# All scores of the next attention pair in one TensorE visit, over six PSUM banks, and four more weight conversions in the first batch

## The chip, the cores and the metric

The kernel runs on one core of one Trainium2 chip. The metric is the device time of one execution in microseconds (us). The engines are TensorE (PE, with its weight loads listed apart as PEld), VectorE (DVE), ScalarE (ACT), GpSimd (POOL) and SyncE (SP, which issues the DMAs).

## The reference

Four batches of eight heads, 576 tokens, head size 64, all float32. The result of the attention, as a matrix of 2304 tokens by 512, goes through a gated feed-forward block:

```python
scores = scale * np.matmul(q, k.transpose(0, 1, 3, 2))        # causal mask, minus row maximum
a = np.exp(scores); a /= a.sum(-1, keepdims=True) + 1e-09
local = np.matmul(a, v)
q_p = phi(q)                                                  # phi(x) = max(x, 0) + exp(min(x, 0))
mem_out = einsum(q_p, M_prev) / (einsum(q_p, z_prev) + 1e-6)
attn = g * mem_out + (1 - g) * local                          # g = sigmoid(beta), one per head
x = attn.transpose(0, 2, 1, 3).reshape(2304, 512)
out = ((x @ w1) * (x @ w2)) @ w3 @ w_out                      # w1, w2: 512x1024, w3: 1024x1024, w_out: 1024x512
```

The weights come to the chip as float64 numbers, seen as pairs of 32-bit words, and are converted to float32 there.

## The kernel before

**Pairs.** Two heads form a pair; there are 16 pairs, four to a batch. The q and k of a pair lie on the 128 partitions as two halves of 64 (`a` = 0 and 1), so a score matmul uses half of the array's rows, one head each. The 576 query tokens are cut into c = 0 (64 rows, both heads together, `s_mm0`) and c = 1 to 4 (128 rows each, for both heads), whose causal rows are 64, 192, 320, 448 and 576 keys long. For each c the scores go to PSUM, are read by DVE (`s_red`, L179: mask added, negative maximum taken, result to the SBUF tile `sm`), go through the exponential on ACT (`s_exp`, L217, which also sums), and are scaled by DVE (`s_norm`, L221 to L226). PE then transposes `sm` (`t_mm`, L236, L257), ACT copies the transposes to `pt` (L267), and PE forms the product with v (`pv_mm`, L283) in the PSUM tile `x`, to which `mem_mm` (L273, L274) has already written the memory part. `fin` (L293 on ACT, L294 on DVE) splits `x` into a high and a low part in `xs`. The memory part needs `mem_a`, `mem_b`, `mem_c` on ACT, DVE and POOL and five transposes on PE (`mem_t`, L162).

**PSUM.** `ps_t` has four banks, used in turn for scores and transposes. `ps_x` is one tile of two banks, which serves the transposes of `mem_t` and the output `x` of a pair. `ps_m` has two banks for the fill described next.

**Fill.** Attention alone leaves PE free for much of the time. So other matmuls are woven in: the string `ORDER` gives the steps of a pair (transposes, product and end of pair p, scores and softmax of pair p + 1), and each `F` in it is a slot in which a generator puts in its share of matmuls. In the first batch the generator is `w_gen` (L413: w3 times w_out). In batches 2 to 4 it is `moe_gen` of the batch before: `gemm1` (L447, twelve matmuls of 288 columns to a PSUM bank, evicted by ACT at L453 and multiplied in by DVE at L456, after which ACT and POOL split the product at L458 and L459) and `gemm2` (L467, 24 matmuls of 512 columns to a bank). The last batch's feed-forward runs alone at the end.

**Conversion.** Forty jobs convert the weights, each by ACT (L315), DVE (L319, L320) and, for w1 and w2, ACT and POOL again (L327, L328). `conv_tick` moves all jobs on by a stage; a slot calls it when `tick_ok` allows. In the first batch it allows jobs up to `limit`; after it, all.

A scheduler orders the instructions of each engine from this program order and priorities; each engine then works through its own list in order and waits on semaphores.

Of the kernel before, what the change touches and what calls it, by code (L numbers as in the profile page):

```python
# [21 lines left out]
    "lqn t2 F "  # L22
    "t3a F "
    "th t3b F "
    "s321 ma F "
    "e3 mb F "
    "n3 t4a F "
    "e2 e1 t4b t5 F "
    "n2 s4 mc F "
    "e4 F "  # L30
    "mm s0 e0 n4 F "
    "pv lq F "
    "fin F "
).split()
# [7 lines left out]
def attention_moe_kernel(  # L42
# [13 lines left out]
    nc = tc.nc  # L56
# [129 lines left out]
    def s_group(p, jobs):  # L186
        t = raw_t[p]
        red = []
        for group in jobs:
            xs = [bank(), bank()]  # L190
            o = 0
            for c, lo, hi in group:
                for a, x in enumerate(xs):
                    r = slice(64 * a, 64 * a + 64)
                    nc.tensor.matmul(x[:, o:o + hi - lo], lhsT=t[r, 0, 128 * c - 64:128 * c + 64], rhs=t[r, 1, lo:hi], start=True, stop=True)  # L195
                    red.append((c, a, x[:, o:o + hi - lo], lo, hi))
                o += hi - lo
        for c, a, x, lo, hi in red:
            s_red(p, c, a, x, lo, hi, lo == 0)

    def s_mm4(p):
        s_group(p, [[(4, 0, 288)], [(4, 288, 576)]])

    def s_mm321(p):
        s_group(p, [[(3, 0, 448)], [(2, 0, 320), (1, 0, 192)]])

    def s_mm0(p):
        x = bank()
        nc.tensor.matmul(x[:, 0:64], lhsT=qd, rhs=raw_t[p][:, 1, 0:64], start=True, stop=True)
        s_red(p, 0, 0, x[:, 0:64], 0, 64)  # L210

# [85 lines left out]
    def conv_stages(k, src, dh, dl):  # L297
# [15 lines left out]
        def scale():  # L313
            box["p"] = dh() if k < 24 else o_p.tile([128, n], F32, tag="o", name="wp")
            nc.scalar.activation(out=box["p"], in_=f32(box["raw"][:, :, 1]), func=ACTF.Prelu, scale=2.0 ** -111, alpha=-(2.0 ** 32))  # L315
# [50 lines left out]
    limit = [28]  # L366
# [149 lines left out]
    def pair_step(p, F):  # L516
# [13 lines left out]
            s4=(nx, lambda: s_mm4(p + 1)),  # L530
            s321=(nx, lambda: s_mm321(p + 1)),
            s0=(nx, lambda: s_mm0(p + 1)),
# [6 lines left out]
            n2=(nx, lambda: s_norm(p + 1, 4, 8)),  # L539
            n4=(nx, lambda: (s_norm(p + 1, 0, 2), s_norm(p + 1, 8, 9))),  # L540
# [45 lines left out]
    s_mm321(0)  # L586
# [3 lines left out]
    s_norm(0, 2, 8)  # L590
    conv_tick()
    s_mm4(0)
    s_mm0(0)
    s_exp(0, 4)
    s_exp(0, 0)
    s_norm(0, 0, 2)
    s_norm(0, 8, 9)
# [49 lines left out]
```

## Time and profile before

| what | value |
|---|---|
| median of 3 runs | 594.22 us (592.11, 594.22, 594.63) |
| the profiled execution | 592.49 us, span 590.7 us from the first to the last instruction |
| mean granted TensorE clock | 0.974 of full speed |
| busy | PE 557.9 us, PEld 441.2, DVE 288.5, ACT 279.7, POOL 125.5 |

The profile shows one execution, the 592.49 us one; its span leaves out about 1.8 us before the first and behind the last instruction. A PE line in the timeline joins neighbouring matmuls of one line; "x12" counts records, and a float32 score matmul leaves two records (two passes). Record ends are modelled, so the distance from start to start tells more than a length.

### The profile page before, as it was taken

The page shows a single profiled execution, that of the slowest core. Times are in us where ns is not written, and L with a number is a line of the kernel's source. Part 1 is how long each engine was busy: PE and PEld are TensorE (multiplying, and loading weights), DVE is VectorE, ACT ScalarE, POOL GpSimd, SP SyncE. Part 2 cuts the span into 40 slices and gives each one's busy share as a digit, 9 for nine tenths or more (in the row PEclk, how much of TensorE's full clock was granted, in tenths as well). Part 3 has the DMA queues.
Part 4 walks back from the last instruction along what each step waited for, and adds up shares of the span by engine and source line. Part 5 has one row for each costly group of instructions (what it writes and reads, how often), then busy time and mean ns, then how long its engine had stood idle before and what let it go on. Part 6 is the DMA issues. An engine that isn't in the chain of part 4 may idle for free.

```text
span 590.7 us, 9323 instructions
## 1 busy us (share of the span) xinstructions
PE 557.9 (94%) x3440; PEld 441.2 (75%) x3440; DVE 288.5 (49%) x910; ACT 279.7 (47%) x723; POOL 125.5 (21%) x153
## 2 busy tenths in 40 slices
PE   4499979999699999999999999999999999999997
PEld 2344445456589798878897888788887988898995
DVE  5967978765844536263636262626363531111111
ACT  4745857456735355544544464425452743121220
POOL 1201232114612022211330122103120311121220
PEclk8689999999899999999999999999999999999999
DMA  7983453506111121113111203040303000000001
GB/s 272 403 346 94 148 182 125 177 20 173 36 43 50 62 68 32 59 29 110 41 54 34 91 4 89 22 132 6 88 6 122 2 23 19 18 2 19 19 1 53
DMA packets 23070, 48.31 MB, mean 82 GB/s; under 512 B 6897, under 2 KB 13041, under 8 KB 21489
## 3 DMA queue, kind: packets, MB, share of 16 engines
q1 hardware_dynamic: 23024, 47.72, 24.3%
q8 instruction: 27, 0.44, 0.3%
q14 instruction: 19, 0.15, 0.1%
HBM read 43.00 MB, written 4.72 MB: 81 GB/s over the span
## 4 chain that ended last, share of the span: by engine, by line
PE 77%; DVE 11%; ACT 6%; POOL 2%; DMA 2%; issue 2%; SPq 0%; DVEq 0%; ACTq 0%
PE m L447 31%; PE m L467 17%; PE x L283 7%; PE s L236 7%; PE m L413 6%; PE s L195 6%; PE x L274 2%; ACT sm L217 2%; DVE sm L179 2%; DVE sm L226 2%; PE x L162 1%; POOL e L143 1%; DVE qn L141 1%; DMA wst<-w_out 1%; DVE wp L320 1%
## 5 line engine op out<-in xcount | busy, mean ns | idle before, releaser
L447 PE MATMUL m<-xs,wsp 128*128 128x288 f32 x1536 | 230.1, 302 | 5.2 <-DVE a L456 5.0
L447 PEld LDWEIGHTS m<-xs,wsp 128*128 128x128 f32 x1536 | 209.4, 190 | 11.5 <-DVE a L456 5.5
L217 ACT ACTIVATE sm<-sm,mx 128x448 f32<-128x448 f32 (+2 forms) x144 | 82.8, 576 | 80.5 <-DVE mx L179 80.4
L459 POOL TENSOR_TENSOR ht<-a,ht 128x288 fp32r<-128x288 f32 (+2 forms) x96 | 57.2, 607 | 273.0 <-ACT ht L458 272.9
L467 PE MATMUL m<-wH,ht 128*128 128x512 f32 x288 | 98.5, 402 | 0.0
L267 ACT ACTIVATE pt<-s 128x512 f32<-128x512 f32 (+1 forms) x144 | 65.9, 487 | 32.3 <-PE s L236 26.2
L456 DVE SCALAR_TENSOR_TENSOR a<-m,a 128x288 f32<-128x288 f32 x64 | 29.1, 455 | 97.3 <-PE m L447 97.2
L236 PE MATMUL s<-ident,sm 128*128 128x128 f32 x448 | 68.9, 282 | 4.8 <-DVE sm L226 4.8
L179 DVE CUSTOM_DVE_ANT_0 sm<-s,mask 128x448 f32<-128x448 f32 (+2 forms) x144 | 58.4, 448 | 22.1 <-PE s L195 20.5
L236 PEld LDWEIGHTS s<-ident,sm 128*128 128x128 f32 x448 | 56.8, 146 | 16.0 <-issue 12.5
L413 PE MATMUL m<-wo,w3s 128*128 128x512 f32 x128 | 66.0, 635 | 1.7 <-DVE w3s L320 1.7
L467 PEld LDWEIGHTS m<-wH,ht 128*128 128x128 f32 x288 | 54.1, 188 | 13.4 <-issue 2.6
L195 PE MATMUL s<-raw 64*128 64x288 f32 (+3 forms) x320 | 56.2, 455 | 8.0 <-DMA raw<-qkt 4.4
L226 DVE TENSOR_SCALAR sm<-sm,sums 128x448 f32<-128x448 f32 (+2 forms) x144 | 62.4, 476 | 1.8
L458 ACT ACTIVATE ht<-a 128x288 fp32r<-128x288 f32 (+2 forms) x96 | 31.2, 356 | 56.8 <-DVE a L456 56.8
L467 PE MATMUL m<-wL,ht 128*128 128x512 f32 x144 | 56.4, 392 | 0.0
L195 PEld LDWEIGHTS s<-raw 64*128 64x128 f32 x320 | 30.6, 191 | 32.3 <-issue 11.7
L143 POOL TENSOR_TENSOR e<-qn,z 128x640 f32<-128x640 f32 x16 | 25.2, 1572 | 120.1 <-DVE qn L141 120.1
L283 PE MATMUL x<-pt,v 128*64 128x448 f32 (+4 forms) x384 | 46.7, 392 | 0.0
L283 PEld LDWEIGHTS x<-pt,v 128*64 128x64 f32 x384 | 25.1, 137 | 25.7 <-issue 21.1
L453 ACT ACTIVATE a<-m 128x288 f32<-128x288 f32 x64 | 25.8, 404 | 37.9 <-PE m L447 32.2
L413 PEld LDWEIGHTS m<-wo,w3s 128*128 128x128 f32 x128 | 22.7, 200 | 20.0 <-issue 17.6
(62 smaller groups left out, 427.5 us busy)
## 6 DMA issues: line engine op xcount, KB each, us to landing
raw<-qkt SPq DMA_DIRECT2D x16, 576.0 KB, 3.8
wst<-w3t SPq DMA_DIRECT2D x8, 1024.0 KB, 12.2
wst<-w SPq DMA_DIRECT2D x16, 512.0 KB, 4.4
qn<-qn SPq DMA_DIRECT2D x16, 320.0 KB, 3.0
v<-v SPq DMA_DIRECT2D x32, 160.0 KB, 2.3
out<-o SPq DMA_DIRECT2D x18, 256.0 KB, 2.0
wst<-w_out SPq DMA_DIRECT2D x4, 1024.0 KB, 9.4
z<-z_prev SPq DMA_DIRECT2D x16, 64.0 KB, 2.8
```

Of the source, the lines that this page charges most:

```text
L179: nc.vector.tensor_tensor_reduce(out=sm[a][c][:, lo:hi] if c else sm0[:, 0:64], in0=x, in1=mask[:, S - KE[c] + lo:S - KE[c] + hi] if c els ...
L195: nc.tensor.matmul(x[:, o:o + hi - lo], lhsT=t[r, 0, 128 * c - 64:128 * c + 64], rhs=t[r, 1, lo:hi], start=True, stop=True)
L217: nc.scalar.activation(out=x, in_=x, func=ACTF.Exp, bias=mx, scale=-1.0, accum_out=sums_of(p)[:, k:k + 1])
L226: nc.vector.tensor_scalar(out=x, in0=x, scalar1=sums_of(p)[:, k:k + 1], scalar2=None, op0=ALU.mult)
L236: tr = lambda o, c, a, kc: nc.tensor.transpose(ps[:, o:o + 128], sm[a][c][:, 128 * kc:128 * kc + 128], ident)
L267: nc.scalar.activation(out=d, in_=s, func=ACTF.Copy)
L283: nc.tensor.matmul(x[64 * a:64 * a + 64, 384 + q0:384 + q1], lhsT=vv[:, a, kc], rhs=pt[:, a, o:o + q1 - q0], start=False, stop=(q0 == 0 or ...
L413: nc.tensor.matmul(ps, lhsT=w[:, 128 * kc:128 * kc + 128], rhs=wo[:, 512 * (kc % 2):512 * (kc % 2) + 512], start=(kc == 0), stop=(kc == 7))
L447: nc.tensor.matmul(ps[:, 0:U], lhsT=w[:, i, x, j], rhs=x_t[NC * b + j][:, xx, U * u:U * u + U], start=(k == 0), stop=(k == 11))
L458: nc.scalar.activation(out=hbuf(f, 0)[:, p:p + c], in_=a[:, o:o + c], func=ACTF.Copy)
L459: nc.gpsimd.tensor_tensor(out=hbuf(f, 1)[:, p:p + c], in0=a[:, o:o + c], in1=f32(hbuf(f, 0)[:, p:p + c]), op=ALU.subtract)
L467: nc.tensor.matmul(ps, lhsT=hbuf(f, a)[:, p:p + 128], rhs=b[f], start=(k == 0), stop=(k == 23))
```

## The change

In `ORDER`, the scores of the next pair were computed at three places: `s321` (c = 3, 2, 1 over four banks), `s4` (c = 4 as two times 288 columns over four banks) and `s0`. Now there is one step `ss`, behind `mm`, `pv` and `fin` of the current pair: c = 4 as 512 + 64 columns and c = 3 in the four banks of `ps_t`, and c = 2 and 1 in the two banks of `ps_x` (tile `sx`), which become free when `fin` has read `x`; then `s_mm0`. The exponentials and normalisations of the next pair follow in the six slots from there to the first transposes `t1`, in the order c = 4, 3, 2, 1, 0; the transposes of the current pair are moved together at the front. The prologue for the first pair follows the same order. Apart from this, `limit` goes from 28 to 32, and the jobs k = 26, 27, 30, 31, 34 and 35 take their buffer `wp` from the pool `big` instead of the pool `o`.

```diff
--- before.py
+++ after.py
@@ -19,18 +19,18 @@
 
 ORDER = (
     "lv mt t1 F "
-    "lqn t2 F "
-    "t3a F "
-    "th t3b F "
-    "s321 ma F "
-    "e3 mb F "
-    "n3 t4a F "
-    "e2 e1 t4b t5 F "
-    "n2 s4 mc F "
-    "e4 F "
-    "mm s0 e0 n4 F "
-    "pv lq F "
+    "lqn t2 th F "
+    "t3a t3b F "
+    "t4a F "
+    "t4b t5 F "
+    "mm pv ma F "
     "fin F "
+    "ss lq mb F "
+    "F "
+    "e4 mc F "
+    "n4 e3 F "
+    "n3 F "
+    "e2 e1 e0 n2 F "
 ).split()
 
 
@@ -183,31 +183,27 @@
         )
         stat["mx", p, a, c] = mx
 
-    def s_group(p, jobs):
-        t = raw_t[p]
-        red = []
-        for group in jobs:
-            xs = [bank(), bank()]
-            o = 0
-            for c, lo, hi in group:
-                for a, x in enumerate(xs):
-                    r = slice(64 * a, 64 * a + 64)
-                    nc.tensor.matmul(x[:, o:o + hi - lo], lhsT=t[r, 0, 128 * c - 64:128 * c + 64], rhs=t[r, 1, lo:hi], start=True, stop=True)
-                    red.append((c, a, x[:, o:o + hi - lo], lo, hi))
-                o += hi - lo
-        for c, a, x, lo, hi in red:
-            s_red(p, c, a, x, lo, hi, lo == 0)
-
-    def s_mm4(p):
-        s_group(p, [[(4, 0, 288)], [(4, 288, 576)]])
-
-    def s_mm321(p):
-        s_group(p, [[(3, 0, 448)], [(2, 0, 320), (1, 0, 192)]])
-
     def s_mm0(p):
         x = bank()
         nc.tensor.matmul(x[:, 0:64], lhsT=qd, rhs=raw_t[p][:, 1, 0:64], start=True, stop=True)
         s_red(p, 0, 0, x[:, 0:64], 0, 64)
+
+    def s_all(p):
+        t = raw_t[p]
+        lay = []
+        for a in range(2):
+            lay.append([bank(), bank()])
+        xx = ps_x.tile([128, 1024], F32, tag="x", name="sx")
+        red = []
+        for i, o, c, lo, hi in ((0, 0, 4, 0, 512), (1, 0, 4, 512, 576), (1, 64, 3, 0, 448), (2, 0, 2, 0, 320), (2, 320, 1, 0, 192)):
+            for a in range(2):
+                y = xx[:, 512 * a + o:512 * a + o + hi - lo] if i == 2 else lay[a][i][:, o:o + hi - lo]
+                r = slice(64 * a, 64 * a + 64)
+                nc.tensor.matmul(y, lhsT=t[r, 0, 128 * c - 64:128 * c + 64], rhs=t[r, 1, lo:hi], start=True, stop=True)
+                red.append((c, a, y, lo, hi))
+        for c, a, y, lo, hi in red:
+            s_red(p, c, a, y, lo, hi, lo == 0)
+        s_mm0(p)
 
     def s_exp(p, c):
         for a in range(2 if c else 1):
@@ -311,7 +307,12 @@
             nc.sync.dma_start(out=t[:, 0:2 * n].bitcast(U32), in_=src.bitcast(U32))
 
         def scale():
-            box["p"] = dh() if k < 24 else o_p.tile([128, n], F32, tag="o", name="wp")
+            if k < 24:
+                box["p"] = dh()
+            elif k < 36 and k % 4 > 1:
+                box["p"] = big.tile([128, n], F32, tag=f"r{4 + k % 4}", name="wp")
+            else:
+                box["p"] = o_p.tile([128, n], F32, tag="o", name="wp")
             nc.scalar.activation(out=box["p"], in_=f32(box["raw"][:, :, 1]), func=ACTF.Prelu, scale=2.0 ** -111, alpha=-(2.0 ** 32))
 
         def join():
@@ -363,7 +364,7 @@
     tick = [0]
     nload = [0]
     w_done = [0]
-    limit = [28]
+    limit = [32]
 
     def tick_ok():
         k = tick[0]
@@ -527,17 +528,15 @@
             t1=(1, lambda: t_mm(p, "1")),
             th=(1, lambda: t_mm(p, "h")),
             t5=(1, lambda: t_mm(p, "5")),
-            s4=(nx, lambda: s_mm4(p + 1)),
-            s321=(nx, lambda: s_mm321(p + 1)),
-            s0=(nx, lambda: s_mm0(p + 1)),
+            ss=(nx, lambda: s_all(p + 1)),
             e4=(nx, lambda: s_exp(p + 1, 4)),
             e3=(nx, lambda: s_exp(p + 1, 3)),
             e2=(nx, lambda: s_exp(p + 1, 2)),
             e1=(nx, lambda: s_exp(p + 1, 1)),
             e0=(nx, lambda: s_exp(p + 1, 0)),
             n3=(nx, lambda: s_norm(p + 1, 2, 4)),
-            n2=(nx, lambda: s_norm(p + 1, 4, 8)),
-            n4=(nx, lambda: (s_norm(p + 1, 0, 2), s_norm(p + 1, 8, 9))),
+            n2=(nx, lambda: s_norm(p + 1, 4, 9)),
+            n4=(nx, lambda: s_norm(p + 1, 0, 2)),
             lq=(p + 2 < NP, lambda: load_qk(p + 2)),
             mm=(1, lambda: mem_mm(p)),
             pv=(1, lambda: pv_mm(p)),
@@ -583,18 +582,15 @@
         nc.vector.tensor_copy(out=gis[:, :, 2 * k:2 * k + 2], in_=gp)
     for a in range(2):
         nc.vector.tensor_copy(out=gis[64 * a:64 * a + 64, :, 8], in_=gp[64 * a:64 * a + 64, :, a])
-    s_mm321(0)
+    s_all(0)
+    s_exp(0, 4)
+    conv_tick()
+    s_norm(0, 0, 2)
     for c in (3, 2, 1):
         s_exp(0, c)
         conv_tick()
-    s_norm(0, 2, 8)
-    conv_tick()
-    s_mm4(0)
-    s_mm0(0)
-    s_exp(0, 4)
     s_exp(0, 0)
-    s_norm(0, 0, 2)
-    s_norm(0, 8, 9)
+    s_norm(0, 2, 9)
     load_qk(1)
     mem_a(0)
     mem_b(0)
```

What the scheduler makes of it, on the two engines at which most of the waits of this part are: first PE, from one score visit to the next of a pair beside the feed-forward block (s are the banks of `ps_t`, m those of `ps_m`, numbers in tile names are buffers). Before:

```order
L195 MATMUL s<-raw 128x448 [waits DMAHW4_49,Activation_49]
L195 MATMUL s<-raw 128x448 [waits Activation_49]
L195 MATMUL s<-raw 128x320 [waits PE_49,Activation_49]
L195 MATMUL s<-raw 128x320 [waits Activation_49]
L195 MATMUL s<-raw 128x192 x2
...
L195 MATMUL s<-raw 128x288 [waits DVE_49]
L195 MATMUL s<-raw 128x288 [waits Activation_49] x3
...
L209 MATMUL s<-raw,qd 128x64 [waits DMAHW6_49,DMAHW5_49,DVE_49]
```

Two visits of the row halves, and the 64-column matmul of c = 0 alone, each between fill (the rows left out are L447, L467 and transposes). After, around the visit before pair 9:

```order
L448 MATMUL m<-xs,wsp 128x288 x5
L202 MATMUL s<-raw 128x512 [waits DMAHW6_49,PE_49]
L202 MATMUL s<-raw 128x512 [waits PE_49]
L202 MATMUL s<-raw 128x64 [waits PE_49] x2
L202 MATMUL s<-raw 128x448 x2
L202 MATMUL sx<-raw 128x320 [waits DVE_49]
L202 MATMUL sx<-raw 128x320
L202 MATMUL sx<-raw 128x192 x2
L188 MATMUL s<-raw,qd 128x64 [waits DMAHW7_49,DMAHW0_49,DVE_49]
L448 MATMUL m<-xs,wsp 128x288 x18
L448 MATMUL m<-xs,wsp 128x288 [waits Activation_49]
L448 MATMUL m<-xs,wsp 128x288 x11
```

All ten row-half matmuls and the c = 0 matmul now stand in one place, 21 L448 behind the last product with v (L279); the first one on `sx` waits for DVE, and the fill behind has a wait for ACT after 18 matmuls, at the bank that L454 has to read (L454 is L453 of before, L448 is L447).

Second, ACT in a pair beside the feed-forward block. Before:

```order
L217 ACTIVATE sm_110,sums<-sm_110,mx 128x448 [waits DVE_49]
L217 ACTIVATE sm_114,sums<-sm_114,mx 128x448 [waits DVE_49]
L217 ACTIVATE sm_109,sums<-sm_109,mx 128x320 [waits DVE_49]
L453 ACTIVATE a<-m 128x288 [waits PE_49,Pool_49]
L217 ACTIVATE sm_113,sums<-sm_113,mx 128x320 [waits DVE_49]
L217 ACTIVATE sm_108,sums<-sm_108,mx 128x192 [waits DVE_49]
L217 ACTIVATE sm_112,sums<-sm_112,mx 128x192 [waits DVE_49]
L458 ACTIVATE ht<-a 128x288 [waits DVE_49]
L267 ACTIVATE pt<-s 128x4x128 [waits PE_49]
```

The exponentials of c = 3, 2 and 1 (sm_110, sm_114, sm_109, sm_113, sm_108, sm_112) stood together, with the eviction L453 after three of them; those of c = 4 and 0 came later, behind other evictions and copies. After:

```order
L459 ACTIVATE ht<-a 128x288 [waits DVE_49]
L213 ACTIVATE sm_111,sums<-sm_111,mx 128x576 [waits DVE_49]
L213 ACTIVATE sm_110,sums<-sm_110,mx 128x448 [waits DVE_49]
L213 ACTIVATE sm_115,sums<-sm_115,mx 128x576 [waits DVE_49]
L213 ACTIVATE sm_114,sums<-sm_114,mx 128x448 [waits DVE_49]
L213 ACTIVATE sm_109,sums<-sm_109,mx 128x320 [waits DVE_49]
L454 ACTIVATE a<-m 128x288 [waits PE_49,Pool_49]
L213 ACTIVATE sm_113,sums<-sm_113,mx 128x320 [waits DVE_49]
L213 ACTIVATE sm_108,sums<-sm_108,mx 128x192 [waits DVE_49]
L213 ACTIVATE sm_112,sums<-sm_112,mx 128x192 [waits DVE_49]
L213 ACTIVATE sm_107,sums<-sm_107,mx 128x64 [waits DVE_49]
L459 ACTIVATE ht<-a 128x288 [waits DVE_49]
```

All nine exponentials (L213) now follow each other, c = 4 (sm_111, sm_115) among the first, and one eviction L454 stands among them, behind five.

## Rows read from the trace of the kernel before

**Rows 1.** The page: PE's busy line, and the chain that ended last.

```profile
PE 557.9 (94%) x3440; PEld 441.2 (75%) x3440; DVE 288.5 (49%) x910; ACT 279.7 (47%) x723; POOL 125.5 (21%) x153
...
PE 77%; DVE 11%; ACT 6%; POOL 2%; DMA 2%; issue 2%; SPq 0%; DVEq 0%; ACTq 0%
```

**Rows 2.** Table by windows: start:end, length, busy us of each engine, clock.

```profile
115.79:141.28 25.49, 25.49 (x118) 13.38 (x116) 16.18 (x51) 14.99 (x37) 5.72 (x4) 1.00 0.22 62
141.28:508.60 367.32, 361.93 (x2451) 305.58 (x2450) 170.35 (x565) 179.93 (x482) 81.87 (x100) 0.99 0.18 54
```

**Rows 3.** Waits of PE: us in total, times, longest.

```profile
PE m L447 <- DVE a L456: 5.0, 2, 4.2
```

**Rows 4.** PE timeline, first batch: start us, us, instructions, [idle before].

```profile
29.40 8.06 PE L413 MATMUL m<-wo,w3s 128*128 128x512 f32 x12 [1.70 <-DVE w3s L320]
...
55.16 0.74 PE L162 MATMUL x<-ident,qn 128*128 128x128 f32 x5 [1.22 <-DVE xs L294]
...
85.61 0.98 PE L162 MATMUL x<-ident,qn 128*128 128x128 f32 x5 [3.51 <-DVE xs L294]
...
87.23 1.92 PE L413 MATMUL m<-wo,w3s 128*128 128x512 f32 x2
...
89.59 1.02 PE L413 MATMUL m<-wo,w3s 128*128 128x512 f32 x2
...
104.58 0.92 PE L195 MATMUL s<-raw 64*128 64x288 f32 x4 [1.73 <-ACT pt L267]
```

**Rows 5.** PE timeline, first MoE block beside attention, at the first wait.

```profile
159.50 2.53 PE L447 MATMUL m<-xs,wsp 128*128 128x288 f32 x9 [4.20 <-DVE a L456]
```

**Rows 6.** The chain of waits that leads to that place.

```profile
154.19 1.02 DVE wp L320
...
156.29 1.23 DVE wp L319
```

**Rows 7.** PE timeline of a steady pair beside gemm1.

```profile
217.13 1.83 PE L447 MATMUL m<-xs,wsp 128*128 128x288 f32 x12
218.89 1.89 PE L195 MATMUL s<-raw 64*128 64x448 f32 x12
...
228.31 1.24 PE L195 MATMUL s<-raw 64*128 64x288 f32 x8
...
233.34 0.33 PE L209 MATMUL s<-raw,qd 128*128 128x64 f32 x2
```

**Rows 8.** Weight loads of the middle visit of that pair.

```profile
228.31 0.79 PEld L195 LDWEIGHTS s<-raw 64*128 64x128 f32 x8 [0.17 <-issue]
```

**Rows 9.** DVE timeline of that pair: reads of scores, normalisation.

```profile
220.07 0.62 DVE L179 CUSTOM_DVE_ANT_0 sm<-s,mask 128x448 f32<-128x448 f32 x1
...
222.53 0.16 DVE L221 SCALAR_TENSOR_TENSOR sums<-sums,gis 128x2 f32<-128x2 f32 x1
...
224.44 0.17 DVE L221 SCALAR_TENSOR_TENSOR sums<-sums,gis 128x4 f32<-128x4 f32 x1 [0.33 <-ACT sm L217]
...
224.86 1.49 DVE L226 TENSOR_SCALAR sm<-sm,sums 128x320 f32<-128x320 f32 x4
...
229.10 0.46 DVE L179 CUSTOM_DVE_ANT_0 sm<-s,mask 128x288 f32<-128x288 f32 x1 [0.95 <-PE s L195]
```

**Rows 10.** ACT timeline of that pair: exponentials and one eviction.

```profile
220.73 0.67 ACT L217 ACTIVATE sm<-sm,mx 128x448 f32<-128x448 f32 x1 [0.54 <-DVE mx L179]
...
222.05 0.55 ACT L217 ACTIVATE sm<-sm,mx 128x320 f32<-128x320 f32 x1
...
222.60 0.39 ACT L453 ACTIVATE a<-m 128x288 f32<-128x288 f32 x1
...
223.44 0.44 ACT L217 ACTIVATE sm<-sm,mx 128x192 f32<-128x192 f32 x1
...
230.41 0.78 ACT L217 ACTIVATE sm<-sm,mx 128x576 f32<-128x576 f32 x1 [1.70 <-DVE mx L179]
...
234.26 0.35 ACT L217 ACTIVATE sm<-sm,mx 128x64 f32<-128x64 f32 x1
```

## The prediction

> **What bounds the kernel now.** I read the page first: PE is busy for 557.9 of 590.7 us, and the chain that ended last runs 77% on PE and 11% on DVE [rows 1]. So the time falls only if PE has less to do, or waits less, and there are 33 us of waiting in all. The table by windows tells where: from 141 to 509 us, where the feed-forward block fills the gaps, PE idles 5.4 of 367 us, and one wait of 4.2 us, for the DVE step L456, is most of that [rows 2, 3]. The last quarter of the first batch, 115.8 to 141.3 us, shows no idle PE at all [rows 2], so the first batch can starve PE but need not. The timeline then gives the single waits of the first batch: 1.22 and 3.51 us before the memory transposes L162 (for DVE's L294, which frees the tile `x`), 1.73 us in the middle of a score visit (for ACT's copy L267, which frees a bank), 1.70 us before the first fill [rows 4]. The wait of 3.51 us is followed by a slower clock: the fill matmul behind it took 1.92 us where the next but one took 1.02 [rows 4]. The wait of 4.2 us at 159.5 us likewise: the nine matmuls behind it took 2.53 us [rows 5], while twelve of the same kind take 218.89 - 217.13 = 1.76 us in a steady pair [rows 7], 0.147 each, so that nine should take 1.3. The reader should see from this that almost every pair beside the feed-forward block is already full: what the change can lose there (new waits) is more than what it can win.
>
> **Fewer visits to the row halves (gain).** The matmuls and columns are the same: 960 columns (192 + 320 + 448) and 576 for each half before, 1536 in one visit now. The two visits took 1.89 and 1.24 us [rows 7]. The slope is 0.65 / 384 = 1.69 ns a column, and what does not scale is 1.89 - 1.62 = 0.27 us a visit. One visit fewer saves 0.27 us a pair at best, and 15 pairs save 4.0. Against this, c = 4 was 288 + 288 and is now 512 + 64. By the slope the 64 columns take 0.11 us, but they are four records (two halves, two passes), and eight weight loads of this shape took 0.79 us [rows 8], 0.10 each. If each of the four needs its load in turn, the piece takes 0.40 us, 0.29 more, and nothing is won (+0.3 in all). The loads can run under the 512-column matmuls ahead, so I lean to the good end: 0.20 a pair, **-3.0 us** (bounds -4.0 and +0.3). The c = 0 matmul (0.33 us with its modelled end [rows 7]) is only moved.
>
> The Trainium skill, "TensorE: Matmul & The Clock Gate", section "LDWEIGHTS (loading the stationary operand)", has a load cost its columns over 1.2 per ns, whatever the rows. For the 128 columns here that is 107 ns, and the row's 0.10 agrees; by that rule alone the short pieces would eat the gain.
>
> **The chain from the scores to the first transposes (loss).** Before, the softmax of a pair was spread over most of the pair before it, and PE's transposes found it done. Now everything from the scores to `t1` lies in six slots. With T = 0 at the start of the visit:
> - DVE's first read waits for 512 columns. For 288 it came 229.10 - 228.31 = 0.79 us after the visit's start [rows 7, 9]; 224 columns more make 1.17.
> - Six reads of 1920 columns took 222.53 - 220.07 = 2.46 us [rows 9], 1.28 ns a column. All 3136 columns (two heads of 1536, and 64) take 4.0 us and end at 5.2. The first c = 4 tile is whole after 512 + 512 + 64 columns, at 2.6.
> - ACT's exponentials take 0.78, 0.67, 0.55 and 0.44 us for 576, 448, 320 and 192 columns, and 0.35 for 64 [rows 10]: twice the four and the last are 5.2 us, with one eviction L454 among them (0.39 us [rows 10]) they end at 8.2.
> - DVE's last normalisation: two small steps, 224.86 - 224.44 = 0.42 us, then 1.49 for the two tiles of c = 2 and the two of c = 1 [rows 9], which `t1` needs: 10.1.
>
> PE has, from T = 0: the visit, 0.27 + 1536 x 1.69 ns = 2.86 us, about 0.2 for c = 0, then fill, and some 0.5 us of memory transposes. Beside gemm1 there are 66 fill matmuls (9.7 us) in six of the pairs' transitions, so `t1` is reached at 13.3 and does not wait. In one transition there are 24 of 512 columns; by columns I estimate 0.26 us each, 6.3, and `t1` is reached at 9.9: a wait of some 0.5 us. The rest have more.
>
> But in the six transitions with gemm1 the fill itself can be held up. Behind the visit stand 18 matmuls (2.6 us), so at 5.7 the next needs a bank that L454 on ACT must have read, and L454 stands behind five exponentials: 2.6 + 0.78 + 0.67 + 0.78 + 0.67 + 0.55 + 0.39 = 6.4. PE waits 0.7 us, six times 4.2. Queued behind L454 on ACT are four more exponentials, and behind these the normalisation. With the 0.5 and with what the wait for DVE's products costs elsewhere I take **+5 us** (bounds 0, if ACT starts earlier than worked out here, and +10, if the delay is twice that).
>
> **The first batch (about even).** The fill there is 8 matmuls of about 0.88 us (1.02 us with the modelled end [rows 4]), 7.0 us, so `t1` is reached at 3.1 + 7.0 + 0.5 = 10.6, against 10.1 on a free DVE and ACT. They are not free: the slots carry conversion jobs, whose two DVE steps were 1.02 and 1.23 us long elsewhere [rows 6]. Two or three such steps inside the chain make it 12.1 to 13.7, and PE waits 1.5 to 3.1 us in each of four transitions: 8.8. What goes: 1.22 + 3.51 + 1.73 = 6.5 us of waits [rows 4], since the memory transposes no longer follow `fin` at once and the visit no longer competes with transposes for its banks. The clock's dip (1.92 - 1.02 = 0.9) I leave as it is, since a wait of 3 us stays. The first fill came after a wait of 1.70 us for a conversion [rows 4]; the transposes of c = 4 now stand ahead of it and can lie in that time: -1.7. Together **+0.6 us** (bounds -6 and +6). The wait that could take the place of the one for L294 is that of the visit's last part on `sx`, which needs the same L294; it comes about 2 us later on PE than L162 did, so of 3.51 us up to 1.5 can stay.
>
> **Four more conversion jobs in the first batch (gain).** The chain to the wait at 159.5 us passes through conversion steps on DVE, 1.02 and 1.23 us [rows 6], between which the score reads and L456 stand in line. With four jobs more done ahead, in a stretch where PE did not wait at all (115.8 to 141.3 us [rows 2]) and DVE was busy for 16.2 of 25.5 us [rows 2], these steps are out of the line. At best the 4.2 us and the slow stretch behind it (2.53 - 1.3 = 1.2) go, 5.4; the memory chain, on DVE and POOL in the same place, would be late next. I take **-4.5 us** (bounds -5.4 and 0).
>
> **The sum** is -3.0 + 5 + 0.6 - 4.5 = -2 us on the profiled execution of 592.5, so 590.5. That execution is 1.7 us under the median of 594.2. A difference of 0.5% (3 us, 591.2 to 597.2 around the median) is about what a measurement of this kernel can tell from no change, so the forecast lies just on the faster side.
>
> **Rivals.**
> 1. *The new waits do not come* (for: the last quarter of the first batch shows that DVE and ACT can keep up; against: nine exponentials in a row are 5.2 us of ACT). Without the 5 us, and with half of the 8.8, the time is 590.5 - 5 - 4.4 = 581.
> 2. *Nothing comes of it*: the short pieces cost what their loads cost (+3.3 against my term), or the wait at 159.5 us stays (+4.5), since the memory chain sets it and not the conversion. 593.8 to 595.
> 3. *Slower, by one mechanism*: evictions and reads of the fill stand behind the block of reads and exponentials on ACT and DVE, for longer than I worked out, in the ten tight places (six transitions with gemm1, four in the first batch). For: each engine works in its own order, and L454 of the changed order stands behind five exponentials. Against: ACT is at 47% and DVE at 49% of the span [rows 1]. At 1.5 us more in each, 590.5 + 15 = 605.5. It decides from (597.2 - 590.5) / 10 = 0.67 us more in each; below that it ends as no change.
>
> To the third: the Trainium skill, "TensorEngine Tiling (Array Packing)", section "PSUM Bottleneck", says that tiling speeds up TensorE but not the evacuation of PSUM, which may become the bottleneck; it advises both ScalarE and VectorE for it. It speaks against a larger visit, since the six banks are all read by DVE. The rows here cannot show it, as no visit of before filled more than four.
>
> **How the numbers follow.** The forecast (587 to 593) has a chance of 0.36, the first rival 0.16, the second 0.25, the third 0.23. Two thirds of the forecast's own chance lie under 591.2, as do all of the first rival's and a little of the second's: faster 0.43. Above 597.2 lies the third rival, and some of its mild form counts as no change, but a little is added for clock dips behind the new waits: slower 0.25. Within 0.5%: 0.32. The range goes from the first rival's time to halfway into the third's: 582 to 601. The likeliest case's own range is 587 to 593.
>
> **What would show it.** One score visit a pair, of some 2.9 us from its first 512-column matmul to c = 0. No waits of L162 for L290 (L294 of before) or of the scores for ACT's copies in the first batch. In their place waits of the transposes L232 of c = 1 for DVE's normalisation L222, of 1.5 to 3 us, four times. Waits of L448 for ACT's L454 (and for DVE's L457) of some 0.7 us, six times. A first wait in the feed-forward block that is well under 4.2 us. The prediction is wrong if the visits take 3.1 us or more (first term), if L448 waits 1.5 us or more at each transition (third rival), or if the 4.2 us stay.

## The result, and the profile after

The changed kernel took 585.67 us (median of 4 runs, 585.04 to 586.22) where the kernel before took 593.63 on the same chip: a ratio of 0.9876, interval 0.9862 to 0.9891. A second measurement on another chip, told below, gave 0.9894 (0.9877 to 0.9911). So the change is worth 1.1 to 1.2%, 6 to 8 us, of which I had forecast 2 to 4. The profiled execution took 586.22 us, 6.3 less than the profiled one of before.

The page of the changed kernel, PE's busy line, beside [rows 1]:

```profile
PE 547.8 (94%) x3440; PEld 435.7 (75%) x3440; DVE 275.6 (47%) x878; ACT 276.0 (47%) x723; POOL 127.1 (22%) x153
```

PE is busy 10.1 us less for the same 3440 matmuls with the same columns in all, while its idle time rose from 32.8 to 36.6 us (span less busy). So the gain is not one of waiting less: the matmuls themselves take less time, and a part of that is given back in new waits. A part of the busy time is clock: between the starts of pairs 4 and 5 (table below) PE was busy for 34.0 us at a mean granted clock of 0.91 before, and for 31.2 us at 1.00 after. The waits of PE (total, times, longest; three of the seven lines are left out) beside [rows 3]:

```profile
PE s L232 <- DVE sm L222: 13.3, 4, 10.0
PE sx L202 <- DVE xs L290: 4.7, 2, 4.5
PE m L448 <- ACT a L454: 4.5, 7, 0.8
PE x L162 <- POOL qn L156: 4.4, 2, 2.8
```

The waits of L448 for DVE are gone and seven waits for ACT have come, of at most 0.8 us, as worked out. (10 of the 13.3 us of L232 are in the prologue, where the transposes waited 4.8 and 3.3 us before.) The memory transposes L162 wait 4.4 us for POOL's L156, in the first two pairs, where they waited 1.5 us before; no term of the forecast had this. To see where the time went, the best ruler is the first memory transpose (L162) of each pair, since the work up to it is nearly the same in both kernels. A lead in the first batch is good to about 1 us: in a second profiled execution of the changed kernel pair 3 starts 1.15 us earlier, at 114.62. The table gives its start in the two timelines:

| pair | before, us | after, us | lead of the change, us |
|---|---|---|---|
| 0 | 26.37 | 27.36 | -0.99 |
| 1 | 55.16 | 53.35 | 1.81 |
| 2 | 85.61 | 78.65 | 6.96 |
| 3 | 115.79 | 115.77 | 0.02 |
| 4 (first beside gemm1) | 141.28 | 140.56 | 0.72 |
| 5 | 179.73 | 174.42 | 5.31 |
| 10 | 330.10 | 323.65 | 6.45 |
| 15 | 485.20 | 479.03 | 6.17 |

Three things are to be read from it. A lead of 7 us is won in the first two pairs and lost in one, between pairs 2 and 3. 4.6 us are won at once where the feed-forward block starts. And after that, from pair 5 to 15, the lead hardly moves: 0.9 us in ten pairs.

The loss between pairs 2 and 3, in PE's timeline:

```profile
81.04 0.67 PE L232 MATMUL s<-ident,sm 128*128 128x128 f32 x4 [1.68 <-DVE sm L222]
...
102.70 2.08 PE L202 MATMUL sx<-raw 64*128 64x320 f32 x8 [4.46 <-DVE xs L290]
105.91 0.69 PE L188 MATMUL s<-raw,qd 128*128 128x64 f32 x2 [1.13 <-DVE mx L179]
106.39 9.54 PE L414 MATMUL m<-wo,w3s 128*128 128x512 f32 x16
```

The second part of the visit (`sx`) waits 4.46 us for L290, then c = 0 waits 1.13 us. What follows runs at a slower clock. In the table by windows (start:end, length, busy us, then the granted clock, the share of the DMA engines and GB/s; a clock of 1.00 is 2.4 GHz):

```profile
102.70:106.39 3.69, 2.56 (x10) 1.67 (x11) 3.66 (x6) 1.11 (x3) 1.39 (x1) 0.50 0.71 210
106.39:115.77 9.38, 9.38 (x18) 3.99 (x19) 9.26 (x41) 6.45 (x20) 0.00 (x0) 0.74 0.70 220
```

the clock is 0.50 of full (1.2 GHz) right behind the wait and 0.74 on the mean over the fill that follows: the c = 2 and 1 matmuls took 2.08 us, 1.03 in a steady pair (below), and the 16 records of fill 9.54 us. The wait of the transposes L232 for DVE, which I had put at 1.5 to 3.1 us four times, is 1.68 us here, and 1.45 and 0.22 at two other places.

A steady pair without waits, from one L162 to the next, with the visit and the fill (here gemm2, L468; L467 before) around it; and the same pair of the kernel before, with its two visits and a group of transposes between fill:

```profile
174.42 0.71 PE L162 MATMUL x<-ident,qn 128*128 128x128 f32 x5
...
192.46 0.39 PE L468 MATMUL m<-wH,ht 128*128 128x512 f32 x1
192.78 2.10 PE L202 MATMUL s<-raw 64*128 64x512 f32 x12
194.72 1.03 PE L202 MATMUL sx<-raw 64*128 64x320 f32 x8
195.68 0.43 PE L188 MATMUL s<-raw,qd 128*128 128x64 f32 x2
195.92 0.48 PE L468 MATMUL m<-wH,ht 128*128 128x512 f32 x1
196.24 0.40 PE L468 MATMUL m<-wL,ht 128*128 128x512 f32 x1
...
204.43 0.71 PE L162 MATMUL x<-ident,qn 128*128 128x128 f32 x5
```

```profile
179.73 0.71 PE L162 MATMUL x<-ident,qn 128*128 128x128 f32 x5
...
188.45 1.89 PE L195 MATMUL s<-raw 64*128 64x448 f32 x12
190.27 0.67 PE L447 MATMUL m<-xs,wsp 128*128 128x288 f32 x3
...
193.32 0.40 PE L467 MATMUL m<-wH,ht 128*128 128x512 f32 x1
193.56 0.60 PE L236 MATMUL s<-ident,sm 128*128 128x128 f32 x4
...
197.52 1.24 PE L195 MATMUL s<-raw 64*128 64x288 f32 x8
198.69 0.50 PE L467 MATMUL m<-wH,ht 128*128 128x512 f32 x1
...
210.20 0.71 PE L162 MATMUL x<-ident,qn 128*128 128x128 f32 x5
```

The pair takes 30.01 us where it took 30.47. That is the visit's saving with everything around it. From start to start, the visit to the row halves takes 195.68 - 192.78 = 2.90 us, and the two of before 190.27 - 188.45 = 1.82 and 198.69 - 197.52 = 1.17, together 2.99, so hardly any of the 0.46 us shows in the visits' own records. Where it is, the experiments tell.

A pair beside gemm1, PE first, then ACT:

```profile
222.58 2.10 PE L202 MATMUL s<-raw 64*128 64x512 f32 x12
...
225.72 4.20 PE L448 MATMUL m<-xs,wsp 128*128 128x288 f32 x30
230.53 5.03 PE L448 MATMUL m<-xs,wsp 128*128 128x288 f32 x36 [0.61 <-ACT a L454]
```

```profile
225.29 0.78 ACT L213 ACTIVATE sm<-sm,mx 128x576 f32<-128x576 f32 x1 [2.92 <-DVE mx L179]
...
230.09 0.38 ACT L454 ACTIVATE a<-m 128x288 f32<-128x288 f32 x1
```

This is the wait that was worked out: the visit starts at 222.58, ACT's first exponential at 225.29 (2.7 us later; I had 2.6), L454 at 230.09 behind seven exponentials, and PE goes on at 230.53. The place was another than worked out (30 fill matmuls ahead of the wait and not 18, seven exponentials and not five), the size nearly the same. The modelled wait is 0.61 us, and this transition costs about 0.75 us against a stream of matmuls without a gap.

### The profile page after: what moved, and what is told of

It is laid out like the page before. It is cut to its first block, busy times and chain, and to the rows that moved or that the text cites. A ratio compares the mean times of both kernels' runs of the same rounds, so it can differ in the third digit from the quotient of the medians.

```text
span 584.4 us, 9283 instructions
## 1 busy us (share of the span) xinstructions
PE 547.8 (94%) x3440; PEld 435.7 (75%) x3440; DVE 275.6 (47%) x878; ACT 276.0 (47%) x723; POOL 127.1 (22%) x153
## 4 chain that ended last, share of the span: by engine, by line
PE 76%; ACT 11%; DVE 7%; issue 3%; POOL 2%; DMA 1%; SPq 0%; DVEq 0%; ACTq 0%
PE m L448 31%; PE m L468 17%; PE x L279 7%; PE s L232 7%; ACT sm L213 7%; PE m L414 5%; PE s L202 3%; PE x L270 2%; POOL wsp L329 1%; DVE sm L179 1%; PE x L162 1%; DVE sm L222 1%; DMA wst<-w_out 1%; DVE wp L321 1%; PE sx L202 1%
## 5 line engine op out<-in xcount | busy, mean ns | idle before, releaser
L448 PE MATMUL m<-xs,wsp 128*128 128x288 f32 x1536 | 223.4, 299 | 4.5 <-ACT a L454 4.5
L448 PEld LDWEIGHTS m<-xs,wsp 128*128 128x128 f32 x1536 | 206.8, 188 | 7.0 <-ACT a L454 6.1
L213 ACT ACTIVATE sm<-sm,mx 128x576 f32<-128x576 f32 (+2 forms) x144 | 82.2, 573 | 45.4 <-DVE mx L179 45.4
L468 PE MATMUL m<-wH,ht 128*128 128x512 f32 x288 | 94.0, 395 | 0.0
L232 PE MATMUL s<-ident,sm 128*128 128x128 f32 x448 | 62.6, 277 | 13.3 <-DVE sm L222 13.3
L232 PEld LDWEIGHTS s<-ident,sm 128*128 128x128 f32 x448 | 53.5, 143 | 20.2 <-issue 13.9
L414 PE MATMUL m<-wo,w3s 128*128 128x512 f32 x128 | 63.2, 633 | 0.7 <-DVE w3s L321 0.7
L468 PEld LDWEIGHTS m<-wH,ht 128*128 128x128 f32 x288 | 54.1, 188 | 11.2
L468 PE MATMUL m<-wL,ht 128*128 128x512 f32 x144 | 56.2, 390 | 0.0
L179 DVE CUSTOM_DVE_ANT_0 sm<-s,mask 128x512 f32<-128x512 f32 (+2 forms) x80 | 44.0, 567 | 24.1 <-PE s L202 24.1
L222 DVE TENSOR_SCALAR sm<-sm,sums 128x576 f32<-128x576 f32 (+2 forms) x144 | 54.6, 441 | 0.4
L454 ACT ACTIVATE a<-m 128x288 f32<-128x288 f32 x64 | 26.1, 408 | 49.9 <-PE m L448 44.8
L279 PEld LDWEIGHTS x<-pt,v 128*64 128x64 f32 x384 | 25.1, 137 | 29.9 <-issue 24.0
L279 PE MATMUL x<-pt,v 128*64 128x448 f32 (+4 forms) x384 | 46.7, 392 | 0.0
L290 DVE TENSOR_TENSOR xs<-x,xs 128x576 fp32r<-128x576 f32 x16 | 12.1, 757 | 69.0 <-ACT xs L289 69.0
L202 PE MATMUL s<-raw 64*128 64x512 f32 (+2 forms) x192 | 35.8, 506 | 4.3 <-DMA raw<-qkt 4.3
```

The costliest lines, as they stand in the source:

```text
L179: nc.vector.tensor_tensor_reduce(out=sm[a][c][:, lo:hi] if c else sm0[:, 0:64], in0=x, in1=mask[:, S - KE[c] + lo:S - KE[c] + hi] if c els ...
L202: nc.tensor.matmul(y, lhsT=t[r, 0, 128 * c - 64:128 * c + 64], rhs=t[r, 1, lo:hi], start=True, stop=True)
L213: nc.scalar.activation(out=x, in_=x, func=ACTF.Exp, bias=mx, scale=-1.0, accum_out=sums_of(p)[:, k:k + 1])
L222: nc.vector.tensor_scalar(out=x, in0=x, scalar1=sums_of(p)[:, k:k + 1], scalar2=None, op0=ALU.mult)
L232: tr = lambda o, c, a, kc: nc.tensor.transpose(ps[:, o:o + 128], sm[a][c][:, 128 * kc:128 * kc + 128], ident)
L279: nc.tensor.matmul(x[64 * a:64 * a + 64, 384 + q0:384 + q1], lhsT=vv[:, a, kc], rhs=pt[:, a, o:o + q1 - q0], start=False, stop=(q0 == 0 or ...
```

## Experiments

**1. The order alone.** The limit back at 28, the buffers as before:

```diff
-            if k < 24:
-                box["p"] = dh()
-            elif k < 36 and k % 4 > 1:
-                box["p"] = big.tile([128, n], F32, tag=f"r{4 + k % 4}", name="wp")
-            else:
-                box["p"] = o_p.tile([128, n], F32, tag="o", name="wp")
+            box["p"] = dh() if k < 24 else o_p.tile([128, n], F32, tag="o", name="wp")
...
-    limit = [32]
+    limit = [28]
```

> The changed kernel with the limit back at 28 and the buffers of the conversion as before: the new order alone. Two effects of the four jobs are in question: they removed the wait of 4.2 us at the start of the feed-forward block (with the slow stretch behind it, the time between pairs 4 and 5 fell by 4.6 us), and conversion steps stand in front of fin's L289 and L290 where the visit waits 4.46 us for the bank of x between pairs 2 and 3 (the lead lost there is 6.9 us). Theory: both belong to the four jobs and nearly cancel, so this kernel takes 582 to 587 us, without the wait of 4.46 us and with a wait of 3 to 4 us near the first feed-forward matmuls. Rival 1 (the limit is the gain): the wait for x stays, the other one returns, about 590 us. Rival 2 (the order alone feeds the feed-forward block in time): neither wait, about 579 us.

Measured: 587.41 us against 592.27, ratio 0.9917 (0.9898 to 0.9937). The wait for x between pairs 2 and 3 was 2.1 us, not gone, and the lead at pairs 4 and 5 was 3.19 and 5.74 us: without the four jobs the start of the feed-forward block is 2.55 us quicker than in the kernel before. So neither half of my theory holds as it stood: the new order by itself removes about half of the loss at 159.5 us (2.1 us, when a visit's 0.45, measured below, is taken off), so that no single wait of 3 to 4 us returns there, and a wait for x is there without the four jobs. The time lies just above the theory's 587; neither rival came whole, the first having the wait for x right and the second the start of the feed-forward block.

**2. The limit alone.** The same lines changed the other way in the kernel before: its limit to 32, and the six buffers from `big`.

> The kernel before with the limit at 32 and the buffers of the change: the four jobs alone, in the old order. Theory: the wait of 4.2 us at the first feed-forward block goes (-4.6), the waits of the memory transposes for L294 in the first batch, where the same conversion steps stand in front, grow by 2 to 5 us: 590 to 593 us, hardly a change. Rival: no growth of these waits, 589 us or less.

Measured: 590.03 us against 592.27, 0.9959 (0.9939 to 0.9978). At the start of the feed-forward block it gains 2.07 us (lead 0.68 at pair 4, 2.75 at pair 5), and the waits of L162 for L294 did not grow: three, 3.6 us in all, where two were 4.7. But the wait of 4.2 us for L456 is shortened by the four jobs to 3.0 us, and does not go. The rival's reason is right, its size is not reached. 0.9917 x 0.9959 = 0.9876, the ratio of the whole change as first measured, so the two parts may add; experiment 6 leaves it open.

**3. Fewer changes to fill, same visits.** In the kernel before:

```diff
-    "lqn t2 F "
-    "t3a F "
-    "th t3b F "
+    "lqn t2 th F "
+    "t3a t3b F "
+    "F "
...
-    "mm s0 e0 n4 F "
-    "pv lq F "
+    "F "
+    "s0 mm pv e0 n4 lq F "
```

> The kernel before, with its two visits of the row halves where they were, but with two changes between fill and attention matmuls less in each pair: t2 with th and t3a with t3b in one slot each, and s0, mm and pv in one place. In pairs without waits the changed kernel took 30.00 us from one memory transpose to the next where the kernel before took 30.46, although its score visits are only 0.09 us shorter and its c = 0, mm and transposes 0.28 longer; the fill is 0.64 shorter. Theory (each change to fill costs about 0.2 us in the fill, wherever it is, and three were removed): the fill of such a pair falls by about 0.4 us here, the pair by 0.2 to 0.4, the whole by 3 to 5 us. Rival (the gain is that of the score visits alone): no change in the pairs beside the feed-forward block.

Measured: 593.37 us against 592.27, 1.0023 (1.0011 to 1.0035). The pair without waits:

```profile
178.70 0.71 PE L162 MATMUL x<-ident,qn 128*128 128x128 f32 x5
...
209.11 0.71 PE L162 MATMUL x<-ident,qn 128*128 128x128 f32 x5
```

30.41 us, 0.06 less than before. Adding up the distances from start to start in the timeline, the fill of this pair fell by 0.33 us (20.32 to 19.99), but transposes, c = 0 and the memory matmuls grew by 0.27: where two pieces of attention work are put together, the second piece pays at its own start what the fill no longer pays. My theory is refuted; the rival holds.

**4. and 5. The visit cut in two.** c = 4 and 3, a slot of fill, then c = 2, 1 and 0:

```diff
-    "ss lq mb F "
-    "F "
+    "ss mb F "
+    "sr lq F "
```

This is the edit to `ORDER` in the second of the two; the functions behind `ss` and `sr`, not shown, split the visit's matmuls between the two steps.

> The changed kernel with its visit cut in two by one slot of fill (c = 4 and 3, fill, c = 2, 1 and 0), all else as in the change. Theory (one more change to fill costs about 0.2 us in a pair, some of it in the fill): 2 to 4 us in all from this, plus or minus what the later reads of c = 2 and 1 do to the waits; since the wait for x in pair 2 to 3 is met one slot later, up to 3 us of it may go. Rival (the visit itself is what costs, 0.27 us of fixed time in its own records): the score records of a pair grow by 0.27 us and the fill stays.

> The cut visit once more (c = 4 and 3, a slot of fill, c = 2, 1 and 0), with the load of the pair after moved behind the second part, so that both parts read the same q and k. Theory (a visit more costs 0.20 us in the score records and 0.25 in the fill behind it): a pair without waits takes 30.46 us again, as in the kernel before, with 3.1 us of score records; the whole is 5 to 8 us above the changed kernel. Rival (the time of the first cut kernel came from its early load): pairs at 30.0 to 30.2 us, the whole 0 to 3 us above the changed kernel.

The first of these left the load `lq` ahead of the second part, which so multiplied the q and k of the pair after; it took 593.28 us against 592.27, 1.0013 (0.9999 to 1.0027). The second took 590.78 us against 592.92, 0.9964 (0.9951 to 0.9977), on the same chip as the changed kernel's second measurement: 4.5 us more than that, somewhat under the 5 to 8 expected. In both a pair without waits takes 30.46 us; here the second:

```profile
176.14 0.71 PE L162 MATMUL x<-ident,qn 128*128 128x128 f32 x5
...
194.50 2.10 PE L208 MATMUL s<-raw 64*128 64x512 f32 x12
196.54 0.50 PE L475 MATMUL m<-wH,ht 128*128 128x512 f32 x1
196.88 0.40 PE L475 MATMUL m<-wL,ht 128*128 128x512 f32 x1
...
197.82 0.39 PE L475 MATMUL m<-wH,ht 128*128 128x512 f32 x1
198.14 1.13 PE L208 MATMUL sx<-raw 64*128 64x320 f32 x8
199.20 0.43 PE L188 MATMUL s<-raw,qd 128*128 128x64 f32 x2
...
206.60 0.60 PE L162 MATMUL x<-ident,qn 128*128 128x128 f32 x4
```

This is the experiment that decides. 206.60 - 176.14 = 30.46 us: cutting the visit gives back the whole gain of 0.45 us a pair, with nothing else of the order undone but the place of one load. Adding up from start to start, 0.20 us of it are in the visit (2.90 to 3.10) and 0.25 in the fill (19.65 to 19.90). The rows say where. The first part takes 196.54 - 194.50 = 2.04 us where the same matmuls took 1.94 in the uncut visit, the second part 1.06 where it took 0.96. The first L475 (gemm2) matmul behind the first part takes 196.88 - 196.54 = 0.34 us, and the last one ahead of the second part 198.14 - 197.82 = 0.32, where one inside a stretch takes 0.23. Four places, 0.1 us each: about half of the price of a visit lies in the neighbours' records. Not all four are marks of the row halves. Ahead of transposes, which use full rows, the last fill matmul takes 193.56 - 193.32 = 0.24 us, so the 0.32 there is. But behind c = 0, which uses full rows too, the first one takes 196.24 - 195.92 = 0.32, nearly the 0.34 behind the row halves: that part is paid on each return to fill. Experiment 3 shows that full-row pieces which are joined pay it elsewhere; the joined row halves do not. The whole kernel lost 4.5 us and not 15 x 0.45 = 6.8, while its waits for the evictions on ACT were 2.3 us in place of 4.5 and the one of `sx` 3.4 in place of 4.5.

**6. The changed kernel again.**

> The changed kernel once more, beside the next three on one chip, so that they can be set against it. Theory (the order gives 0.8% and the four jobs 0.4%, each by itself, and they add): 0.986 to 0.989 of the kernel before, so 585 to 586 us where that takes 593. Rival (the four jobs add nothing to the new order, as the spans of the profiles say, 584.4 and 584.1 us): 0.990 to 0.993.

Measured: 586.33 us against 592.92, 0.9894 (0.9877 to 0.9911), between the theory and the rival. How much the four jobs add to the new order stays open between 0 and 0.4%; the old order gains 0.4% by them. The starts of the pairs speak for little: from pair 4 to 5 the changed kernel takes 33.9 us and experiment 1 35.9, 2.0 more, but at pair 4 experiment 1 (138.09 us) is ahead of the two profiled executions of the changed kernel (140.56 and 139.42) by 1.3 to 2.5 us. With the new order the jobs cost in the first batch about what they win behind it.

**7. Evictions behind the visit on DVE.**

```diff
-                        nc.scalar.activation(out=a, in_=ps[:, 0:U], func=ACTF.Copy, scale=2.0 ** -8)
+                        if near[0]:
+                            nc.vector.tensor_scalar(out=a, in0=ps[:, 0:U], scalar1=2.0 ** -8, scalar2=None, op0=ALU.mult)
+                        else:
+                            nc.scalar.activation(out=a, in_=ps[:, 0:U], func=ACTF.Copy, scale=2.0 ** -8)
...
+                if t in ("ss", "mt"):
+                    near[0] = t == "ss"
```

The step `ss` sets the mark `near`, `mt` clears it; 15 of the 64 evictions went to DVE, and not half of them.

> The changed kernel with the evictions L454 that are issued between the score visit and the next pair's first memory transposes on DVE in place of ACT (about half of the 64); no work is left out. Theory (L454 waits behind the exponentials on ACT, which costs PE about 0.75 us in each of six or seven transitions): the waits of L448 for ACT, 4.5 us in all, go, DVE has read all scores by then, and the time falls by 3 to 5 us. Rival (the bank comes late because DVE reads and normalises late, so the work only moves): L448 waits for DVE as long, no change within 1 us, or worse where the normalisation of c = 1 is pushed behind.

Measured: 582.07 us against 592.92, 0.9823 (0.9803 to 0.9843), 4.3 us under the changed kernel on the same chip. The waits of the fill in this kernel:

```profile
PE m L449 <- ACT a L458: 0.5, 1, 0.5
PE m L449 <- DVE a L456: 0.4, 1, 0.4
```

0.9 us in place of 4.5, and from pair 5 to 15 the kernel takes 301.7 us, 2.9 less than the changed one and 3.8 less than the one before. This shows that the wait was one for ACT's place in line, not for late work: DVE reads the same bank in time.

**8. The low part of the weights on DVE.** First what the change's trace shows just ahead of its longest wait, on ACT, DVE and POOL:

```profile
98.99 0.63 ACT L328 ACTIVATE wsp<-wp 128x512 fp32r<-128x512 f32 x1 [2.68 <-DVE wp L321]
...
100.07 0.63 ACT L289 ACTIVATE xs<-x 128x576 fp32r<-128x576 f32 x1
```

```profile
93.29 0.68 DVE L321 SCALAR_TENSOR_TENSOR wp<-wst,wp 128x512 uint32<-128x512 uint32 x1
...
95.82 1.46 DVE L320 TENSOR_SCALAR wp<-wp 128x512 uint32<-128x512 uint32 x1 [0.25 <-ACT wp L316]
97.32 1.63 DVE L321 SCALAR_TENSOR_TENSOR wp<-wst,wp 128x512 uint32<-128x512 uint32 x1
...
101.89 0.75 DVE L290 TENSOR_TENSOR xs<-x,xs 128x576 fp32r<-128x576 f32 x1
```

```profile
93.38 1.72 POOL L329 TENSOR_TENSOR wsp<-wp,wsp 128x512 fp32r<-128x512 f32 x1 [1.29 <-ACT wsp L328]
95.75 1.26 POOL L156 TENSOR_TENSOR qn<-qn,n 128x640 f32<-128x640 f32 x1 [0.65 <-DVE n L154]
96.96 1.45 POOL L329 TENSOR_TENSOR wsp<-wp,wsp 128x512 fp32r<-128x512 f32 x1
```

`xs` (L289) has its input when pv ends, at 93.4, and starts on ACT at 100.07, behind conversion steps that wait for DVE's. DVE's L320 takes 1.46 us and its L321 1.63, and they end 0.27 and 0.54 us after the POOL instruction that was running when they started; the L321 at 93.29, which was running when POOL started, took 0.68. The nine long steps of this trace (0.56 us and more) all end so, L320 0.27 to 0.29 us and L321 0.54 to 0.55 after POOL; the longest takes 1.76 us. (The 2.1 us of the expectation below are two steps that the timeline joins in one line.) So the edit:

```diff
-            nc.gpsimd.tensor_tensor(out=dl(), in0=box["p"], in1=f32(dh()), op=ALU.subtract)
+            nc.vector.tensor_tensor(out=dl(), in0=box["p"], in1=f32(dh()), op=ALU.subtract)
```

> The changed kernel with the low part of the converted weights (L329, sixteen times, 1.3 to 1.7 us on POOL) on DVE in place of POOL; no work is left out. In the first batch DVE's conversion steps, 0.42 and 0.68 us by themselves, take 1.5 to 2.1 us where they meet a POOL instruction, and end about when that ends. Theory (the wait of 4.46 us for the bank of x between pairs 2 and 3, and what follows it, comes from DVE being held by POOL): DVE's steps L320 and L321 go to 0.4 to 0.7 us nearly everywhere, the wait falls below 2 us, and the time falls by 2 to 5 us. Rival (DVE has simply too much to do there, and 0.7 us more for each job makes it worse): the wait stays or grows, and the time rises by up to 3 us.

Measured: 581.20 us against 592.92, 0.9812 (0.9797 to 0.9827), 5.1 us under the changed kernel. Two of the waits, and three DVE steps and a POOL instruction of the same stretch:

```profile
PE s L188 <- DVE mx L179: 3.0, 2, 2.4
...
PE sx L202 <- DVE xs L290: 0.2, 1, 0.2
```

```profile
97.25 0.43 DVE L320 TENSOR_SCALAR wp<-wp 128x512 uint32<-128x512 uint32 x1
97.71 1.63 DVE L321 SCALAR_TENSOR_TENSOR wp<-wst,wp 128x512 uint32<-128x512 uint32 x1
...
103.46 0.69 DVE L321 SCALAR_TENSOR_TENSOR wp<-wst,wp 128x512 uint32<-128x512 uint32 x1
```

```profile
97.42 1.37 POOL L156 TENSOR_TENSOR qn<-qn,n 128x640 f32<-128x640 f32 x1 [3.81 <-DVE n L154]
```

The wait of `sx` for L290 is 0.2 us, though DVE has more to do. A wait of 2.4 us for c = 0's bank stands in the same visit instead, and the rest is won. The steps are back at 0.43 and 0.69 us where POOL does nothing; the L321 at 97.71 met POOL's L156, took 1.63 us and ended 0.55 after it. DVE took on 11.8 us of work (the sixteen L329), and its busy time rose by 1.2 us, from 275.6 to 276.8. What is not separated: L329 itself is shorter on DVE, so the next job's L316 on ACT also waits less for it (1.6 us in place of 5.2). How the 5.1 us divide between the two is open.

**9. Both.**

> The changed kernel with both: evictions L454 between the score visit and the next memory transposes on DVE, and the low part of the converted weights (L329) on DVE. Theory (two separate waits, one beside the feed-forward block and one in the first batch): the gains add, 0.990 of the changed kernel for the first and 0.991 for the second, so 0.970 to 0.975 of the kernel before, about 577 us. Rival (DVE becomes what is waited for, where both put work on it): no better than the better of the two alone, 0.980 to 0.982.

Measured: 577.34 us against 592.91, 0.9739 (0.9726 to 0.9753). The two gains add (0.9823 x 0.9812 / 0.9894 = 0.974). This is the fastest version: 1.5% under the changed kernel, 2.6% under the one before.

## Why the prediction came out too small

**Fewer visits: the step that failed.** "What does not scale is 0.27 us a visit", and "one visit fewer saves 0.27 us a pair at best": I had read the fixed price of a visit from the visit's own records [rows 7] and taken it for all of it. The cut visit shows 0.45 us a pair, 0.2 in the visit and 0.25 in the fill, most of it in the last matmul ahead and the first one behind. For 15 pairs that is 6.8 us, outside my bounds (-4.0 and +0.3), where I had taken 3.0. These 3.8 us are most of what the sum (-2) missed against the profiled executions (-6.3). The mechanism was right, the size was not. And of the visit's own records 0.27 was too much, as the lengths have modelled ends: by starts, 1.82 - 960 x 1.69 ns = 0.20. The rows had it before: the fill between visits is in the same timeline, and the distances from start to start around a visit could have been compared with those inside a stretch. The Trainium skill, "TensorEngine Tiling (Array Packing)", section "Key Properties", states that changing the tiling mode drains TensorE. The rows fit it, with 0.1 us more in the last fill matmul ahead of the row halves and in each part of the cut visit; the draining itself no row shows, and the page gives no price.

**The short pieces.** The 64-column pieces cost something: the two parts of the cut visit take 3.10 us together where the two visits of before took 2.99. 0.11 us a pair lies inside the 0 to 0.29 I had allowed. Against the rule of one load after the other (0.29) the rows decide for less.

**The evictions behind the exponentials: right.** 0.7 us at six places, 4.2 us, was forecast (+5 with the rest); 4.5 us at seven places came. (The wait of `t1` beside gemm2, put at 0.5 us, is 10.1 - 9.9 = 0.2 by the prediction's own numbers; PE waited for none there.) Moving L454 to DVE took 4.3 us off the time. That from pair 5 on the lead moves by only 0.9 us in ten pairs is this: 0.45 us a pair is won and most of it given back at every other pair; with the evictions on DVE the lead grows by 3.8 us there.

**The first batch: near in sum, by luck; wrong in parts.** +0.6 us was forecast. The lead at pair 4 is 0.7 us; four visits fewer give 1.8 us, so everything else up to there cost 1.1. The waits of L162 for L290 and of the scores for ACT's copies went, as forecast. The four waits of `t1` (8.8 us) were far too many: 1.68, 1.45 and 0.22 us came. The 2.9 us more that L162 waits for POOL were not in the sum. The wait of `sx` for L290, for which I had allowed 1.5 us, was 4.46 us and, with its clock, cost the 7 us that had been won. I had taken the conversion steps at their longest where they meet the chain of scores, and at nothing where they stand in front of `fin`. The place was wrong, and what makes the steps long, POOL beside DVE, was not seen.

**The four jobs: near in size, wrong in cause.** -4.5 us at the start of the feed-forward block was forecast and -4.6 came (-5.4, when the visit's 0.45 and two of the new waits for ACT, 1.25 us, are taken out). But the jobs alone give 2.1 and the order alone 2.6 (0.45 of it the visit's), and what the jobs add to the new order in the whole is open between nothing and 0.4%. That the order does it by moving the reads of the next scores out from between the conversion steps and L456 is argued from the instruction order, not tested.

**The rivals.** The third (slower) had its mechanism, at the size worked out and no more. (The Trainium skill, "TensorEngine Tiling (Array Packing)", section "PSUM Bottleneck", which I set beside it, says that emptying PSUM may become the bottleneck. The runs bear that out in part: beside gemm1 PE waited not for DVE's reads of the six banks, but for ACT's eviction of another bank, behind the exponentials.) The first (no new waits) did not come, but its time, 581 us, was reached by experiment 8, which took one of the waits away. The second did not come either: the short pieces cost 0.11 us, and the wait of 4.2 us went.

## What to carry to other kernels

The price of a visit to the row halves lies on both sides of the switch: read it from a stretch before and behind, with the distance from start to start, not from the switched instructions alone. An eviction that frees a bank for the main stream should not stand in line behind a block of work for the next step; if the engine's order cannot be moved, give it to another engine that is done by then. And count what two engines cost each other: here sixteen steps moved from POOL to DVE, 11.8 us of work, made DVE busy for only 1.2 us more.

## What was not expected of the hardware

DVE steps that meet a POOL instruction: L320 and L321 take 0.4 and 0.7 us alone and up to 1.76 us there, and the long ones end 0.27 to 0.29 (L320) and 0.54 to 0.55 us (L321) after POOL's instruction. Moving POOL's sixteen L329 (1.3 to 1.8 us each) to DVE, where they take 0.68 us each at the median, made the kernel 5 us faster. Which resource the two share was not tried.

One more visit of TensorE to the row halves between fill costs 0.45 us, about 0.1 us at each of four edges, and putting two different kinds of full-row work side by side saves nearly nothing (experiment 3: 0.33 us less in the fill, 0.27 more in the pieces that were joined).
